# Padding a one-column constant from 4 to 128 bytes, so that the tiles behind it start on multiples of 128 bytes

## The chip, the cores and the metric

The kernel runs on one NeuronCore of a Trainium2 chip. What counts is device time in microseconds, as the median of the runs shown. The profile is of one further execution of the same program, so that execution has a time of its own. TensorE does the matmuls (PE, its weight loads PEld), VectorE (DVE) and ScalarE (ACT) do the arithmetic on whole tiles, GpSimd (POOL) a few normalisations and accumulating stores, and SyncE (SP) issues the other transfers.

## What is computed

Strided and local attention over 8 batches, 8 heads, 576 tokens and a head dimension of 64, and on its result a gated two-layer network with 4608 tokens, 512 model columns and 2048 hidden columns:

```python
scores = (q @ k.T) / sqrt(64)          # per batch and head
mask   = (0 <= i - j < 32) for heads 0..3
         (i >= j and i % 32 == j % 32) for heads 4..7
attn   = softmax(where(mask, scores, -1e9))
x      = (attn @ v) laid out as [4608 tokens, 512]
h      = x @ w_in                       # 512 -> 2048
g      = h * erf(softplus(h))
out    = g @ w_out                      # 2048 -> 512
```

## The kernel before, in words

The work is cut into 12 chunks of 384 tokens. For each chunk and each of 16 blocks of 128 hidden columns, `ftile` issues the first layer (`mm1`, line 678: 12 matmuls of 128x128 by 128x384 into `h`), a chain of ScalarE and VectorE steps for the gate (`n1` to `prod`, lines 686, 683 and 713), the split of the result into a high and a low part (`ghi` on ScalarE, line 716, and `glo` on VectorE, line 719), and the second layer (`mm2`, line 750: 9 matmuls of 128x128 by 128x512 into `o`). Both layers use the fp32r type with high and low parts, so each product is the sum of three matmuls. In the first layer the weight `pair` is the stationary operand and `xhi` or `xlo` streams past it; in the second `ghi` or `glo` is stationary and a weight `pair` streams. The profile writes the streaming operand first: `h<-xhi,pair` and `o<-pair,ghi`.

The attention of the eight batches (`heads`) is woven into this: scores on TensorE (line 400), softmax on the vector engines, transposes (line 507), the product with v (line 526), and the split of its result into `xhi` and `xlo` (lines 545 and 550). The order of all instructions is set when the program is built, by a planner (`Plan.order`) that looks at estimated durations and written keys, and not at addresses.

At the start the weights come in as 64-bit words of 4096 bytes per partition (`load` in `weight`, transfers `words<-w_in` and `words<-w_out`), beside the q, k and v of the first batches, which borrow the slots of weights that are needed later. While the first data comes in, a few matmuls on the constants (`warm`, line 863) keep TensorE occupied.

Memory in each partition of SBUF is handed out pool by pool, in the order in which tiles are asked for. The first pool, `cpool`, holds `xhi`, `xlo`, `ident`, `con` and last `con_e`; behind it lie `apool` (q, k, v, softmax tiles), `mpool` (`a`, `b`, `ghi`, `glo`, `ob`) and `wpool` (weights). `con_e` is one zero per partition: GpSimd sets it (line 793), and ScalarE takes its exponential (line 796) at the very start. No other instruction reads it.

Of the kernel before, what the change touches and what calls it, by code (L numbers as in the profile page):

```python
# [8 lines left out]
F32 = mybir.dt.float32  # L9
# [3 lines left out]
AF = mybir.ActivationFunctionType  # L13
# [5 lines left out]
P = 128  # L19
# [247 lines left out]
def attention_moe(  # L267
# [12 lines left out]
    nc = tc.nc  # L280
    PSUM = bass.MemoryType.PSUM

    cpool = ctx.enter_context(tc.tile_pool(name="cpool", bufs=1))
# [8 lines left out]
    xlo = [cpool.tile([P, RING], F32R, name=f"xlo{c}") for c in range(NCC)]  # L292
    ident = cpool.tile([P, P], F32, name="ident")
    con = cpool.tile([P, NCON], BF16, name="con")
    con_e = cpool.tile([P, 1], F32, name="con_e")
    mask_l = con[:, :320]
    mask_s = con[:, 320:384].rearrange("p (u q) -> p u q", u=1)
    ident_b = con[:, 384:]
# [491 lines left out]
        yield nc.sync.dma_start(ident, ident_f)  # L790

    def zero():
        yield nc.gpsimd.memset(con_e, 0.0)

    def first_exp():
        yield nc.scalar.activation(con_e, con_e, AF.Exp)

    o_con = [plan.add("sp", 0.35, -20.0, load_consts)]
    o_ident = plan.add("sp", 0.2, KI, load_ident)
    o = plan.add("pool", 0.1, -20.0, zero)  # L800
    plan.add("act", 1.6, -18.0, first_exp, [o])
    o_ps, order_o, stored = [None] * NTT, [None] * NTT, {}

# [161 lines left out]
```

## Time and profile before

| | |
|---|---|
| Median of the three runs | 931.43 us (lowest 930.68) |
| Profiled execution | 933.05 us, span 931.3 us |
| Mean granted TensorE clock | 0.993 |
| PE busy | 909.7 us, 98% of the span |
| DVE busy | 686.7 us, 74% |
| ACT busy | 653.4 us, 70% |
| POOL busy | 60.9 us, 7% |
| Moved by DMA | 68.86 MB in 23421 packets |

Three runs are in the list; one of them took 2283.8 us and stands far from the other two and from the profiled execution.

How to read the lines that follow: a group of instructions has its source line, engine, operation, the tile written, an arrow and the tiles read, then partitions by columns for output and input, the count, the busy time in us and the mean duration of one in ns, and last the idle time of the engine ahead of these instructions with what ended it. Matmuls run in a pipeline, so one may last longer than the step from its start to the start of the next. The span in slices gives a digit per fortieth of the span, 23.3 us each: 9 means busy for 90% or more.

### The profile page before, as it was taken

Reading aid. Unit: us, or ns where it says so; the run is one execution under the profiler, and the core shown is the slowest. Engines: PE = TensorE matmul, PEld = TensorE weight load, DVE = VectorE, ACT = ScalarE, POOL = GpSimd, SP = SyncE. Lnnn points to the kernel's source line nnn. Section 1 sums busy time; section 2 is a strip of 40 time slices with the busy share of each in tenths; the row PEclk is TensorE's granted clock in tenths of the full one; section 3 lists DMA queues with packets and bytes.
Section 4 is the critical chain, followed back from the end, with each engine's and each line's share of the span. In section 5 each row is a group of like instructions: output and inputs, shape, how many; then the busy total and the mean of one; then the engine's idle time right before and its main releaser. Section 6 shows DMA issues by size and latency. Waiting matters only on the chain.

```text
span 931.3 us, 20134 instructions
## 1 busy us (share of the span) xinstructions
PE 909.7 (98%) x8166; PEld 809.6 (87%) x8169; DVE 686.7 (74%) x1352; ACT 653.4 (70%) x1476; POOL 60.9 (7%) x59
## 2 busy tenths in 40 slices
PE   5789999999999999999999999999999999999998
PEld 4678888898888889988888899998898899999997
DVE  5999999996757766669886876667876666666664
ACT  5687887887776767667666666766766766766765
POOL 2200012110101100001110100000100000000000
PEclk9799999999999999999999999999999999999999
DMA  9994124321313010013312300002300200000000
GB/s 336 391 362 154 62 57 73 61 34 48 78 58 86 30 64 35 27 57 105 99 56 92 124 17 1 34 1 73 135 1 30 70 1 1 34 1 0 34 1 35
DMA packets 23421, 68.86 MB, mean 74 GB/s; under 512 B 2592, under 2 KB 3232, under 8 KB 23328
## 3 DMA queue, kind: packets, MB, share of 16 engines
q1 hardware_dynamic: 20736, 62.86, 18.9%
q0 software_dynamic: 2592, 4.72, 3.6%
q8 instruction: 64, 1.05, 0.5%
q14 instruction: 29, 0.24, 0.1%
HBM read 53.41 MB, written 14.16 MB: 73 GB/s over the span
## 4 chain that ended last, share of the span: by engine, by line
PE 90%; DVE 4%; ACT 3%; issue 1%; DMA 1%; SPq 0%; POOL 0%; ACTq 0%; POOLq 0%
PE h L678 41%; PE o L750 40%; PE s L400 3%; PE x L526 3%; PE t L507 2%; PE s L526 1%; DMA qk<-qk_loc 1%; ACT b L686 1%; DVE a L683 1%; DVE b L683 1%; ACT a L686 1%; PE s L507 1%; DVE glo L719 1%; ACT sm L472 0%; DVE h L713 0%
## 5 line engine op out<-in xcount | busy, mean ns | idle before, releaser
L750 PE MATMUL o<-pair,ghi 128*128 128x512 f32 x1152 | 361.4, 395 | 0.2 <-ACT ghi L716 0.2
L678 PE MATMUL h<-xhi,pair 128*128 128x384 f32 x1536 | 302.4, 339 | 0.6 <-DVE glo L719 0.6
L678 PEld LDWEIGHTS h<-xhi,pair 128*128 128x128 f32 x1536 | 271.4, 188 | 16.5 <-DVE glo L719 2.6
L686 ACT ACTIVATE b<-b 128x384 f32<-128x384 f32 x384 | 200.4, 522 | 77.2 <-DVE b L683 73.8
L750 PEld LDWEIGHTS o<-pair,ghi 128*128 128x128 f32 x1152 | 209.8, 188 | 32.4 <-ACT ghi L716 0.7
L750 PE MATMUL o<-pair,glo 128*128 128x512 f32 x576 | 224.8, 390 | 0.0
L683 DVE SCALAR_TENSOR_TENSOR a<-h,a 128x384 f32<-128x384 f32 x192 | 106.3, 553 | 83.3 <-ACT a L686 82.8
L678 PE MATMUL h<-xlo,pair 128*128 128x384 f32 x768 | 164.4, 336 | 0.0
L686 ACT ACTIVATE a<-h 128x384 f32<-128x384 f32 x192 | 93.5, 487 | 100.9 <-PE h L678 100.2
L683 DVE SCALAR_TENSOR_TENSOR a<-a,h 128x384 f32<-128x384 f32 x192 | 105.5, 549 | 68.9 <-ACT b L686 68.9
L713 DVE TENSOR_TENSOR h<-b,h 128x384 f32<-128x384 f32 x192 | 107.0, 557 | 46.2 <-ACT b L686 45.8
L678 PEld LDWEIGHTS h<-xlo,pair 128*128 128x128 f32 x768 | 136.0, 188 | 0.0
L750 PEld LDWEIGHTS o<-pair,glo 128*128 128x128 f32 x576 | 108.1, 188 | 23.7 <-DVE glo L719 0.3
L686 ACT ACTIVATE a<-a 128x384 f32<-128x384 f32 x192 | 100.3, 523 | 26.6 <-DVE a L683 26.1
L719 DVE TENSOR_TENSOR glo<-h,ghi 128x384 fp32r<-128x384 f32 x192 | 105.7, 550 | 11.7 <-ACT ghi L716 10.2
L716 ACT CAST ghi<-h 128x384 fp32r<-128x384 f32 x192 | 90.5, 471 | 29.1 <-DVE h L713 15.1
L683 DVE SCALAR_TENSOR_TENSOR b<-b,a 128x384 f32<-128x384 f32 x192 | 108.7, 566 | 1.0
L686 ACT ACTIVATE b<-a 128x384 f32<-128x384 f32 x192 | 101.0, 526 | 4.4
L498 POOL TENSOR_TENSOR sm<-sm,r 128x768 f32<-128x768 f32 (+3 forms) x36 | 45.0, 1249 | 435.3 <-DVE r L491 330.9
L436 DVE TENSOR_REDUCE mx<-s 128x12 f32<-128x768 f32 (+3 forms) x37 | 28.8, 784 | 10.6 <-PE s L413 10.3
L766 ACT COPY ob<-o 128x512 f32<-128x512 f32 x54 | 31.0, 588 | 2.7 <-PE o L750 2.2
L526 PEld LDWEIGHTS x<-pt,v 64*64 64x64 f32 x1392 | 24.4, 135 | 6.9 <-issue 4.4
(49 smaller groups left out, 511.4 us busy)
## 6 DMA issues: line engine op xcount, KB each, us to landing
out<-ob SPq DMA_DIRECT2D x36, 256.0 KB, 2.0
v<-v_loc SPq DMA_DIRECT2D x13, 640.0 KB, 4.1
words<-w_in SPq DMA_DIRECT2D x16, 512.0 KB, 8.6
words<-w_out SPq DMA_DIRECT2D x16, 512.0 KB, 9.1
qk<-qk_loc SPq DMA_DIRECT2D x13, 592.0 KB, 3.8
qk<-qk_str SPq DMA_DIRECT2D x12, 608.0 KB, 3.8
v<-v_str SPq DMA_DIRECT2D x16, 384.0 KB, 3.3
out<-ob POOLq DMA_DIRECT2D x18, 256.0 KB, 4.6
```

The source lines that it names most:

```text
L436: yield nc.vector.tensor_reduce(out=mx[:, parts[i], :units], in_=wide(of(s, i)), axis=mybir.AxisListType.X, op=ALU.max)
L498: yield (nc.gpsimd if pool_norm else nc.vector).tensor_tensor(out=d, in0=d, in1=spread(rc, i), op=ALU.mult)
L507: yield nc.tensor.transpose(bank(t, h)[:, 128 * w : 128 * w + 128], sm[:, h, c : c + 128], ident)
L526: yield nc.tensor.matmul(bank(px, m)[h * D : (h + 1) * D, a * n : (a + 1) * n], values(rows, (2 * a + h) * D), pt[rows, h, c : c + n], sta ...
L678: yield nc.tensor.matmul(ph[:, :CH], win[4 * s + cc][:, w, fs], x[cc][:, c0 : c0 + CH], start=(i == 0), stop=(i == len(terms) - 1))
L683: yield nc.vector.scalar_tensor_tensor(out=out, in0=in0, scalar=scalar, in1=in1, op0=op0, op1=op1)
L686: yield nc.scalar.activation(dst, src, func, bias=bias[i], scale=scale)
L713: yield nc.vector.tensor_tensor(out=ph[:, :CH], in0=bb.tile, in1=ph[:, :CH], op=ALU.mult)
L716: yield nc.scalar.copy(ghi.tile, ph[:, :CH])
L719: yield nc.vector.tensor_tensor(out=glo.tile, in0=ph[:, :CH], in1=ghi.tile.bitcast(F32), op=ALU.subtract)
L750: yield nc.tensor.matmul(po.tile, g[:, ts], wout[f][:, w], start=(f == first_f and i == 0), stop=(f == last_f and i == 2),)
L766: yield nc.scalar.copy(ob.tile, po.tile)
```

## The change

`con_e` is declared with 32 columns of four bytes, and its two users take the first column, as before:

```diff
-    con_e = cpool.tile([P, 1], F32, name="con_e")
+    con_e = cpool.tile([P, 32], F32, name="con_e")
...
-        yield nc.gpsimd.memset(con_e, 0.0)
+        yield nc.gpsimd.memset(con_e[:, :1], 0.0)
...
-        yield nc.scalar.activation(con_e, con_e, AF.Exp)
+        yield nc.scalar.activation(con_e[:, :1], con_e[:, :1], AF.Exp)
```

The order of instructions is the same on every engine. The addresses are not: four bytes took 32 in the pool, now they take 128, and everything behind `con_e` stands 96 bytes further on. From the two built programs, byte address within the partition:

| Tile | before | past a multiple of 128 | now | past a multiple of 128 |
|---|---|---|---|---|
| `xhi` (first), read by the first layer | 16512 | 0 | 16512 | 0 |
| `ident` | 53376 | 0 | 53376 | 0 |
| `con` | 53888 | 0 | 53888 | 0 |
| `con_e` | 54912 | 0 | 54912 | 0 |
| `sm` (first) | 54944 | 32 | 55040 | 0 |
| `mx` (first, second buffer) | 61088, 61152 | 32, 96 | 61184, 61248 | 0, 64 |
| `qk` (first) | 61216 | 32 | 61312 | 0 |
| `a` (first) | 83616 | 32 | 83712 | 0 |
| `ghi` (first) | 89760 | 32 | 89856 | 0 |
| `glo` (first) | 92832 | 32 | 92928 | 0 |
| first weight slot (`words`, `pair`) | 95904 | 32 | 96000 | 0 |

All other tiles behind `con_e` go from 32 to 0 as well, but for the second buffer of `r`, which goes from 96 to 64 like that of `mx`. The weight slots, 4096 bytes each, stood 160 bytes past a multiple of 256 and now stand on one; `con` stands 128 past a multiple of 256 in both kernels. Tiles in PSUM stay where they were.

## The prediction

> **What bounds the kernel now.** I read the page from the top: busy shares first, then the span in slices, then the chain that ended last.
>
> ```profile
> PE 909.7 (98%) x8166; PEld 809.6 (87%) x8169; DVE 686.7 (74%) x1352; ACT 653.4 (70%) x1476; POOL 60.9 (7%) x59
> PE   5789999999999999999999999999999999999998
> PEclk9799999999999999999999999999999999999999
> DMA  9994124321313010013312300002300200000000
> PE 90%; DVE 4%; ACT 3%; issue 1%; DMA 1%; SPq 0%; POOL 0%; ACTq 0%; POOLq 0%
> PE h L678 41%; PE o L750 40%; PE s L400 3%; PE x L526 3%; PE t L507 2%; PE s L526 1%; DMA qk<-qk_loc 1%; ACT b L686 1%; DVE a L683 1%; DVE b L683 1%; ACT a L686 1%; PE s L507 1%; DVE glo L719 1%; ACT sm L472 0%; DVE h L713 0%
> ```
>
> TensorE is busy for 98% of the span and is 90% of the chain; its two large matmul groups, the first layer (h, line 678) and the second layer (o, line 750), are 81% of it. Only the first three slices look different: the DMA engines are full there and TensorE is not. The table by stretch gives that in numbers (columns: length, busy time and count for each engine, granted clock, DMA share, GB/s).
>
> ```profile
> 0.00:23.30 23.30, 13.98 (x378) 9.36 (x382) 13.02 (x33) 12.04 (x51) 5.34 (x10) 1.00 0.94 336
> 23.30:46.60 23.30, 18.24 (x429) 15.44 (x421) 21.08 (x49) 15.28 (x64) 4.78 (x6) 0.71 1.03 391
> 46.60:69.90 23.30, 20.89 (x340) 16.95 (x341) 22.57 (x51) 19.01 (x59) 1.94 (x2) 1.00 0.93 362
> 69.90:500.00 430.10, 429.24 (x3895) 383.44 (x3894) 345.90 (x674) 314.68 (x671) 37.89 (x34) 1.00 0.24 66
> 500.00:931.30 431.30, 427.35 (x3143) 384.41 (x3142) 284.15 (x549) 292.44 (x632) 10.94 (x8) 1.00 0.10 35
> ```
>
> TensorE idles 9.32 + 5.06 + 2.41 = 16.8 us in the first 69.9 us, and only 0.86 + 3.95 = 4.8 us in the remaining 861.4 us. So an address can matter to the time in two places: how fast TensorE reads its operands, everywhere, and how fast the DMA engines write, in the first 69.9 us.
>
> **The change, part by part.** No instruction is added, removed or moved on any engine; the memset and the exponential on the constant keep their one column. What changes is where in its partition each tile of the three later pools starts: 32 bytes past a multiple of 128 before, on it now. I call that remainder the phase. The x tiles, ident and con have phase 0 in both kernels, so the kernel before already holds operands of both kinds, and the trace can be asked to compare them.
>
> *TensorE, moving operand.* The first layer streams x (phase 0), the second streams w_out pairs (phase 32). From the steady part, in order of time (start, length, operation):
>
> ```profile
> 801.09 1.55 PE L678 MATMUL h<-xhi,pair 128*128 128x384 f32 x8
> ...
> 803.18 0.62 PE L750 MATMUL o<-pair,ghi 128*128 128x512 f32 x2
> ...
> 805.22 1.55 PE L678 MATMUL h<-xhi,pair 128*128 128x384 f32 x8
> ```
>
> Twelve first-layer matmuls pass from 801.09 to 803.18, 2.09 us or 174 ns each; nine second-layer ones from 803.18 to 805.22, 2.04 us or 227 ns each. The 128 columns more cost 53 ns, or 0.414 ns a column; 384 columns are then 159 ns and 512 are 212 ns, and each kind has about 15 ns left over. The group that streams from phase 0 carries the same surplus as the group that streams from phase 32. Realigning the moving operand is worth 0.
>
> *TensorE, stationary operand.* Here all large matmuls have phase 32 (weight pairs, ghi, glo), so the pair above cannot decide. The small attention matmuls can. The weight loads of line 526 (v, 64 columns) all start at phase 32. The 64-column ones of line 400 (strided queries) start at multiples of 216 bytes from phase 32, and so at phases 0, 8, 16, 32, 40, 48, 56, 80, 88, 96 and 120.
>
> ```profile
> L526 PEld LDWEIGHTS x<-pt,v 64*64 64x64 f32 x1392 | 24.4, 135 | 6.9 <-issue 4.4 <-ACT b L686 0.7 <-ACT pt L513 0.7
> L400 PEld LDWEIGHTS s<-qk 64*64 64x64 f32 x576 | 9.5, 134 | 3.8 <-issue 1.4 <-ACT pt L513 1.2 <-PE o L750 0.7
> L400 PEld LDWEIGHTS s<-qk x1616: 102/107/136, 15.1 to 677.9; 64*32 64x32 f32 x115, 64*64 64x64 f32 x65
> ```
>
> The mean is 134 ns with all phases mixed and 135 ns with phase 32 alone. The third row gives minimum, median and maximum over all loads of that line: none takes over 136 ns, so no phase costs more than a nanosecond over another. Sorted by phase, leaving out the first ten of each group, the 48 loads at phase 0 have a mean of 135.0 ns and those at 16 and 40 of 135.1. I take 0 for this part too. One end stays open: these loads are plain fp32 and 64 columns wide, the large ones are fp32r and 128 wide. The far end is the first rival below.
>
> *VectorE and ScalarE.* The twins are the two splits into high and low parts: xlo and xhi live at phase 0, glo and ghi at phase 32.
>
> ```profile
> L719 DVE TENSOR_TENSOR glo<-h,ghi 128x384 fp32r<-128x384 f32 x192 | 105.7, 550 | 11.7 <-ACT ghi L716 10.2
> L550 DVE TENSOR_TENSOR xlo<-x,xhi 128x320 fp32r<-128x320 f32 x12 | 5.8, 481 | 0.0
> L550 DVE TENSOR_TENSOR xlo<-x,xhi 128x256 fp32r<-128x256 f32 x12 | 5.1, 424 | 6.7 <-ACT xhi L545 6.5
> L716 ACT CAST ghi<-h 128x384 fp32r<-128x384 f32 x192 | 90.5, 471 | 29.1 <-DVE h L713 15.1 <-PE o L750 13.3 <-PE h L678 0.3
> L545 ACT CAST xhi<-x 128x320 fp32r<-128x320 f32 x12 | 5.2, 430 | 0.0
> L766 ACT COPY ob<-o 128x512 f32<-128x512 f32 x54 | 31.0, 588 | 2.7 <-PE o L750 2.2 <-DMA out<-ob 0.3
> ```
>
> On VectorE the aligned rows grow by 57 ns for 64 columns, so 384 aligned columns would take 538 ns, against 550 unaligned: at most 12 ns, 2%, in favour of alignment. On ScalarE the unaligned rows grow by 117 ns for 128 columns, so 320 unaligned columns would take 412 ns, against 430 aligned: the other sign. Neither is a phase effect that I would bill. At most, 2% of VectorE's 4% of the chain (37 us) is 0.8 us; 18 ns of 412 is 4.4%, and on ScalarE's 3% (28 us) that is 1.2 us lost. Both engines wait for others for a quarter of the span, which hides the rest. Taken: 0.
>
> *DMA.* 25 MB land in the first 69.9 us, worked out from the three rates in the stretches above, most of it in tiles that move. Three issues can be compared:
>
> ```profile
> qk<-v_loc SPq DMA_DIRECT2D x3, 128.0 KB, 7.6
> con<-consts SPq DMA_DIRECT2D x1, 128.0 KB, 3.9
> ident<-ident_f SPq DMA_DIRECT2D x1, 64.0 KB, 7.2
> ```
>
> The first two rows are four transfers of 128 packets of 1024 bytes each, three into phase 32 and one into phase 0. Sorted by size, the packet records have a median of 46 ns for both kinds. The 4480 packets of 4096 bytes, all to or from moved tiles, have a median of 159 ns. That is 0.0368 ns a byte and 8.3 ns a packet, and from this line the 512-byte packets of ident (phase 0) should take 27 ns, which is what all 128 of them take. So phase 0 and phase 32 lie on one line. Taken: 0.
>
> [...]
>
> *Sum.* The profiled execution took 933.05 us, 1.75 us beyond its span of 931.3; plus 0 for TensorE, 0 for the vector engines, 0 for DMA, it is 933.05 us. The median of the runs is 931.43 us, 1.6 us (0.17%) lower, and a measurement of this kernel cannot tell less than about 2% from no change. I predict the median, **931.4 us**.
>
> **The rivals.**
>
> *The stationary operand does pay (faster).* The warm-up matmuls are bf16 with everything at phase 0 and 512 columns:
>
> ```profile
> 11.35 1.46 PE L863 MATMUL warm<-con 128*128 128x512 bf16 x6
> L863 PE MATMUL warm<-con x22: 379/379/635, 5.6 to 59.4; 128*128 128x512 bf16 x22
> ```
>
> Six in 1.46 us, the last one 379 ns long: (1460 - 379) / 5 = 216 ns from start to start, 11 ns less than the second layer. If those 11 ns were the price of an unaligned stationary tile, 1536 + 768 + 1152 + 576 = 4032 large matmuls would give back 44 us: 887 us. The counts have these rows:
>
> ```profile
> L750 PE MATMUL o<-pair,ghi 128*128 128x512 f32 x1152 | 361.4, 395 | 0.2 <-ACT ghi L716 0.2
> L678 PE MATMUL h<-xhi,pair 128*128 128x384 f32 x1536 | 302.4, 339 | 0.6 <-DVE glo L719 0.6
> L750 PE MATMUL o<-pair,glo 128*128 128x512 f32 x576 | 224.8, 390 | 0.0
> L678 PE MATMUL h<-xlo,pair 128*128 128x384 f32 x768 | 164.4, 336 | 0.0
> L863 PEld LDWEIGHTS <-con 128*128 128x128 bf16 x25 | 2.6, 106 | 7.7 <-DMA con<-consts 5.6 <-issue 0.8
> L678 PEld LDWEIGHTS h<-xhi,pair 128*128 128x128 f32 x1536 | 271.4, 188 | 16.5 <-DVE glo L719 2.6
> ```
>
> For it: no fp32r matmul with an aligned stationary tile exists here, and the surplus is the same for both layers, which share just that. Against it: the 64-column loads, which do not care; and the last two rows, where a bf16 load takes 106 ns and an fp32r load of as many columns 188 ns. The two kinds differ in how they load whatever their phase, so the type is enough to explain 11 ns.
>
> *The loading stage shrinks (faster, within 2%).* If the 8.3 ns that each packet costs beyond its bytes were the price of its phase, a 4096-byte packet would fall by 8.3 of 159 ns, 5.2%, and the 69.9 us by 3.6 us: 927.8 us. Even with all 16.8 us of idle TensorE gone it is 914.6 us, still within 2%. The 46 ns and the 27 ns speak against it. [...]
>
> *Equal phases collide (slower).* Now x and the weight pairs, which line 678 reads at once, have one phase where they had two. If reads of one phase got in each other's way, all 2304 first-layer matmuls would pay. The nearest price is again the 11 ns between 227 and 216: 25 us, 957 us. It passes 2% (18.6 us) from 8 ns a matmul on. Against it: the second layer already reads two operands of one phase (pair and ghi, both 32), and has no more surplus than the first.
>
> *The change does not do what it says.* Only if the pools did not move; the addresses in the section on the change show that they do. The second buffers of mx and r go from phase 96 to 64, not 0, but they hold 48 bytes for small vector steps.
>
> **How the numbers follow.** No effect: 0.85, at 931.4. A shorter loading stage: 0.08, 914.6 to 929.5. The stationary operand pays: 0.04, 887. Collision: 0.03, 957. The last two alone leave the 2% band: faster 0.04, same 0.93, slower 0.03. The range takes the likeliest case with its bounds: below, the lowest run (930.68) less 3.6 us of loading, 927.1; above, the profiled execution (933.05) plus the 1.2 us of ScalarE and as much scatter as the readings have among themselves (2.4 us), 936.6.
>
> **What would show it.** In the profile after, the first layer should still step by 174 ns and the second by 227 ns, weight loads should last 188 ns, glo 550 ns, ghi 471 ns, and 4096-byte packets 159 ns; the busy shares should agree to a digit. A second-layer step of 216 ns would prove the first rival, a first-layer step over 180 ns the collision, and DMA shares well under 0.93 in the first three slices the loading rival. I am wrong if 128-column fp32r loads know a phase that 64-column ones do not.

## The result, and the profile after

The changed kernel's median is 936.28 us, against 931.53 us for the kernel before on the same chip: ratio 1.0056, 95% interval [1.0036, 1.0075]. It is slower by half a per cent, and clearly so. The ratio is that of the means, without the one run of 2283.8 us of the kernel before. Its profiled execution took 936.42 us, with a span of 934.7 us.

From the page after, busy shares and the span in slices:

```profile
PE 913.7 (98%) x8166; PEld 812.6 (87%) x8169; DVE 687.6 (74%) x1352; ACT 654.2 (70%) x1476; POOL 61.0 (7%) x59
PEclk9799999999999999999999999999999999999999
DMA  9993224321313010013213300002300200000000
```

The first three stretches of the changed kernel:

```profile
0.00:23.30 23.30, 14.98 (x407) 10.04 (x409) 13.60 (x34) 12.31 (x52) 5.48 (x10) 1.00 0.92 341
23.30:46.60 23.30, 17.45 (x482) 15.32 (x485) 21.52 (x50) 16.51 (x66) 4.65 (x5) 0.78 1.03 404
46.60:69.90 23.30, 20.92 (x263) 17.01 (x257) 23.20 (x53) 18.70 (x60) 1.94 (x2) 1.00 0.92 365
```

TensorE is busy for 4.0 us more; the vector engines for 0.9 and 0.8 us. The groups show the same: the operations that I had compared by phase did not move, the matmuls did.

```profile
L750 PE MATMUL o<-pair,ghi 128*128 128x512 f32 x1152 | 363.6, 397 | 0.3 <-ACT ghi L716 0.2
L678 PE MATMUL h<-xhi,pair 128*128 128x384 f32 x1536 | 304.5, 340 | 0.3 <-DVE glo L719 0.3
L678 PE MATMUL h<-xlo,pair 128*128 128x384 f32 x768 | 165.9, 338 | 0.0
L678 PEld LDWEIGHTS h<-xhi,pair 128*128 128x128 f32 x1536 | 273.0, 188 | 15.6 <-DVE glo L719 1.5
L719 DVE TENSOR_TENSOR glo<-h,ghi 128x384 fp32r<-128x384 f32 x192 | 105.8, 551 | 11.8 <-ACT ghi L716 10.4
L716 ACT CAST ghi<-h 128x384 fp32r<-128x384 f32 x192 | 90.7, 472 | 28.9 <-DVE h L713 15.0 <-PE o L750 13.7
```

The place of the loss is the step from one matmul to the next. One block of the changed kernel in order of time:

```profile
803.54 1.57 PE L678 MATMUL h<-xhi,pair 128*128 128x384 f32 x8
804.95 0.86 PE L678 MATMUL h<-xlo,pair 128*128 128x384 f32 x4
805.65 0.63 PE L750 MATMUL o<-pair,ghi 128*128 128x512 f32 x2
806.12 0.39 PE L750 MATMUL o<-pair,glo 128*128 128x512 f32 x1
806.35 0.62 PE L750 MATMUL o<-pair,ghi 128*128 128x512 f32 x2
806.80 0.39 PE L750 MATMUL o<-pair,glo 128*128 128x512 f32 x1
807.02 0.62 PE L750 MATMUL o<-pair,ghi 128*128 128x512 f32 x2
807.48 0.39 PE L750 MATMUL o<-pair,glo 128*128 128x512 f32 x1
807.71 1.57 PE L678 MATMUL h<-xhi,pair 128*128 128x384 f32 x8
```

The twelve first-layer matmuls take 805.65 - 803.54 = 2.11 us, 0.02 more than before. Of the second layer only the first two steps are longer (806.12 - 805.65 = 0.47 us for two, against 806.80 - 806.35 = 0.45 for the next such pair). The block takes 4.17 us instead of 4.13. In the trace's records of single instructions, to the nanosecond, the median of the 128 blocks whose 21 matmuls follow each other with no other matmul between them goes from 4127 to 4160 ns.

The loss builds up evenly. The 21st block starts 1.6 us earlier than before (135.07 against 136.66 us), so the loading stage of this execution was shorter. From there on each of the remaining 171 blocks costs 29 ns more (4590 against 4561 ns, with all that lies between them), 5.0 us. Less 1.6 that is the 3.4 us between the spans.

### The profile page after: what moved, and what is told of

Same layout as the page of the kernel before. It is cut to its first block, busy times and chain, and to the rows that moved or that the text cites. A ratio compares the mean times of both kernels' runs of the same rounds, so it can differ in the third digit from the quotient of the medians.

```text
span 934.7 us, 20134 instructions
## 1 busy us (share of the span) xinstructions
PE 913.7 (98%) x8166; PEld 812.6 (87%) x8169; DVE 687.6 (74%) x1352; ACT 654.2 (70%) x1476; POOL 61.0 (7%) x59
## 4 chain that ended last, share of the span: by engine, by line
PE 86%; issue 7%; DVE 3%; DMA 2%; ACT 1%; SPq 1%; POOL 0%; ACTq 0%; POOLq 0%
PE h L678 39%; PE o L750 39%; PE x L526 3%; PE s L400 3%; PE t L507 2%; DMA qk<-qk_loc 1%; DMA out<-ob 1%; PE s L526 1%; DVE a L683 1%; PE s L507 1%; ACT b L686 0%; DVE b L683 0%; DVE pair L649 0%; DVE glo L719 0%; DVE w L635 0%
```

## Experiments

The steps of a matmul went up although no other engine did more. I held three theories: **(1)** the operand that TensorE streams and the stationary one that it loads at the same time get in each other's way, depending on where both start; **(2)** stationary tiles that start on a multiple of 128 are slow; **(3)** the vector engines' accesses get in the way of TensorE's when their tiles have the phase of x. Loads and matmuls do run at the same time: in the changed kernel PEld is busy for 812.6 us and PE for 913.7 us of a span of 934.7 us. In what follows the *distance* of a layer is the start of its stationary tile less the start of its streamed tile, modulo 256 bytes. It is 32 for the first and 0 for the second layer before, 128 and 0 after. All tiles that one layer uses in a role have the same remainder, since their sizes and slices are multiples of 256 or 512 bytes.

### Moving one set of tiles at a time

The weight slots alone (phase 0; q, k, v and gate tiles stay at 32):

```diff
+    gap = ctx.enter_context(tc.tile_pool(name="gap", bufs=1)).tile([P, 24], F32, name="gap")
     wpool = ctx.enter_context(tc.tile_pool(name="wpool", bufs=1))
```

> Only the weight slots move, from 32 past a multiple of 128 bytes to 0; q, k, v, softmax and gate tiles (ghi, glo among them) stay at 32, x at 0. Theory 1 (x and the first layer's weights, which TensorE reads at once, get in each other's way when they have one phase): first-layer step 175.5 ns instead of 173.5, the first two second-layer steps after it 234 and 233 instead of 228 and 227 as in the changed kernel, about 936 us. Theory 2 (weights at phase 0 are slow whatever x has): the same. Theory 3 (the vector engines' tiles at the phase of x disturb TensorE): 173.5 ns, about 930 us. The loading stage should end 1.5 us earlier in all three if the writes to the weight slots gain from phase 0.

Measured: 1.0114 [1.0099, 1.0128]. First-layer steps went to 175.8 ns, as in the changed kernel (175.5), but all nine second-layer steps grew, to 232.9 ns on average, which no theory had foreseen. No single set of tiles was responsible for a fixed price.

The attention and gate tiles alone (`con_e` with 32 columns, and a gap of 8 columns ahead of `wpool`):

> Only the tiles of attention and gate move to phase 0 (ghi and glo among them); the weight slots stay at 32 past a multiple of 128 (288 instead of 160 past one of 512), x at 0. Theory 1 and theory 2: first-layer step 173.5 ns, about 931.5 us. Theory 3: 175.5 ns, about 936 us. No gain in the loading stage if it comes from the weight slots.

Measured: 1.011 [1.0093, 1.0127]; 176.4 and 231.9 ns. Here x and the weights keep their phases, and the first layer is slower than in any run so far. Phases modulo 128 are not the right quantity; the weights' remainder of 256 changed.

x, ident and con alone (`con_e` asked for ahead of `xhi`, the rest as before), and the same with everything else at phase 0 (24 columns of padding behind `con` besides):

```diff
+    con_e = cpool.tile([P, 1], F32, name="con_e")
     xhi = [cpool.tile([P, RING], F32R, name=f"xhi{c}") for c in range(NCC)]
...
-    con_e = cpool.tile([P, 1], F32, name="con_e")
```

> Only the x tiles, ident and con move, from phase 0 to 32; everything else stays at 32. x and the weights then have one phase, but it is 32 and not 0. Theory 1: first-layer step 175.5 ns, about 937 us. Theory 2: 173.5 ns, 931.5 us. Theory 3 (equal phase of x and the gate tiles): 175.5 ns.

> x, ident and con at phase 32, everything else at 0: the mirror of the kernel before. Theory 1: first-layer step 173.5 ns, and with the earlier end of loading 930 us. Theory 2: 175.5 ns, 936 us. Theory 3: 173.5 ns, 930 us.

Measured: 1.0082 [1.0066, 1.0098] and 1.0038 [1.0025, 1.0051]. With x at 32 the first layer slowed to 175.2 ns, as theory 1 had it, but the second slowed too, to 231.3 ns, though it does not read x. In the mirror layout the weights are at phase 0 and the first layer has its 173.7 ns, which ends theory 2. The second layer has 231.2 ns there, so the time is not that of before.

### How far the pattern reaches

The same gap with 32 columns (weights 128 bytes further), `con_e` with 40 columns (all behind it 128 further), and with 136 columns (512 further):

> Only the weight slots move, by 128 bytes: all tiles keep their remainder of 128 (x 0, the rest 32), but the weights' remainder of 512 goes from 160 to 288. If only remainders of 128 count, steps stay at 173.5 and 227 ns and the time at that of before. If more of the address counts, steps grow, as they did in the run that moved the tiles of attention and gate alone: 176 and 232 ns, about 943 us.

> Everything behind the constant moves by 128 bytes together; remainders of 128 as before, x unmoved. If only remainders of 128 count: time of before, steps 173.5 and 227 ns. If the distance between x and the weights counts beyond 128 bytes: first-layer step up by 2 ns and second-layer steps up after it, 936 us or more.

> Everything behind the constant moves by 512 bytes; remainders of 512 as before. If the pattern repeats within 512 bytes: time of before, within 0.2%, steps 173.5 and 227 ns. If it doesn't (or if any other layout than the one tuned for is worse for a reason that is not the address), slower by about 0.5 to 1%.

Measured: 1.0118 [1.01, 1.0136], 1.0101 [1.0085, 1.0117] and 0.9996 [0.9986, 1.0006]. A shift of 512 bytes changes nothing, one of 128 costs 1%: more of the address than its remainder of 128 counts, and a whole 512 does not.

### TensorE by itself

The loop of the short kernel, with the names of its variables shortened:

```python
for n in (384, 512):
    for m in range(16):
        for s in range(16):
            matmul(mark, half[:, :128], half)             # one bf16 matmul between groups
            for r in range(24):
                matmul(y[:, :n], sta[:, 8*s + 128*(r%4) :][:, :128], mov[:, 8*m + 512*(r%2) :][:, :n])
```

> Leaves out the whole computation: no attention, no gate, nothing on VectorE or ScalarE while TensorE runs. It streams fp32r matmuls of 384 and then 512 columns, each with its own weight load, in groups of 24 at one pair of starts, the streamed operand at 16 starts 32 bytes apart and the stationary one at 16, so 256 pairs for each length, with one bf16 matmul between groups. Theory 1 (the two operands that TensorE reads at once get in each other's way, by where each starts): the step differs between pairs by some ns, as the program's 173.5 to 176 and 227 to 232 ns do, and the map shows after how many bytes it repeats. Theory 3 (reads and writes of the vector engines get in TensorE's way): 173.3 and 226.7 ns for all 256 pairs. Theory 2 (the stationary start alone counts): the step changes along the stationary starts only.

Four groups of it in order of time, 24 matmuls of 512 columns each, with a streamed start of 0; the stationary start goes from 64 to 192, 224 and 256 bytes:

```profile
1156.38 5.95 PE L43 MATMUL y<-mov,sta 128*128 128x512 f32 x24
...
1179.69 5.85 PE L43 MATMUL y<-mov,sta 128*128 128x512 f32 x24
...
1185.42 5.96 PE L43 MATMUL y<-mov,sta 128*128 128x512 f32 x24
...
1191.26 5.83 PE L43 MATMUL y<-mov,sta 128*128 128x512 f32 x24
```

The groups differ by 0.13 us, with nothing else running (one execution, granted clock 1.00). From the records, the mean of the last 15 steps of a group, over the groups of one distance (the very first group left out):

| Distance, bytes | 0 | 32 | 64 | 96 | 128 | 160 | 192 | 224 |
|---|---|---|---|---|---|---|---|---|
| 384 columns, ns | 173.3 | 173.3 | 173.3 to 176.7 | 173.3 | 176 | 177 | 173.3 | 173.3 to 176.9 |
| 512 columns, ns | 226.9 | 233.4 | 233.4 | 234.3 | 232.4 | 233.4 | 228.9 | 233.4 |

All pairs of starts with one distance lie within 0.7 ns of each other, but for the two cells that give a range. So it is the distance that counts, it repeats after 256 bytes, and theory 3 is not needed. In those two cells the distance alone does not decide: at 64, for instance, the groups have 173.3, 174.7 or 176.6 ns, by where the pair starts. None of the layouts here has a first layer at 64 or 224. The first layer after the change (distance 128) and with only the weights moved (128) is at 176, the second layer of the latter (160) at 233.

What this table, made of the last 15 steps of each group, does not give is the second layer at distance 0, which had 227 ns in some programs and 231 in others. So TensorE ran whole blocks of twelve and nine matmuls, for 8 by 8 distances.

> Leaves out the whole computation. TensorE alone runs the kernel's block order, twelve first-layer and nine second-layer matmuls, five blocks for each of 64 pairs of distances (stationary start less streamed start, 0 to 224 bytes in steps of 32, for either layer). If the distances alone decide, each layer's steps are those of the map of single pairs whatever the other layer does: second layer at distance 0 always 226.7 ns. If what ran before also decides (the runs with distance 0 in the second layer had 227 ns in three programs and 231 ns in three others), the second layer at distance 0 has 227 ns after a first layer at 32 or 128 and 231 ns after one at 0, 96 or 160.

Blocks with distances 32 and 0 (before), and with 128 and 0 (after):

```profile
185.40 2.25 PE L47 MATMUL y<-xt,wt 128*128 128x384 f32 x12
187.48 2.20 PE L49 MATMUL o<-wt,gt 128*128 128x512 f32 x9
189.53 2.25 PE L47 MATMUL y<-xt,wt 128*128 128x384 f32 x12
```

```profile
693.13 2.27 PE L47 MATMUL y<-xt,wt 128*128 128x384 f32 x12
695.24 2.22 PE L49 MATMUL o<-wt,gt 128*128 128x512 f32 x9
697.29 2.27 PE L47 MATMUL y<-xt,wt 128*128 128x384 f32 x12
```

Start to start, 4.13 and 4.16 us: the difference of the two kernels, without the kernels. What ran before does count: at distance 0 the second layer has 227 ns after a first layer at 32, 64 or 224 and 228 after one at 128 or 192, but 231 after one at 0, 96 or 160. After a first layer at 128 its steps are 234, 233, 228 and then about 227 ns: the two long steps of the changed kernel, whose second layer is at distance 0 as it was before. My expectation named 0, 96 and 160 rightly; for 128 it had 227.

The records of the single pairs show what the 231 ns are, which their last 15 steps hide. Of the 32 groups with 512 columns at distance 0, 31 are uneven in their first five to nine steps (224 to 236 ns) and only then settle at 227. One begins, after the gap behind the bf16 matmul, with 229, 233, 236, 224, 231, 236, 228, 233 and 231 ns, and stays at 226 or 227 from there on. These are, within a nanosecond, the nine steps that the second layer has in the program with x at 32. So 231 ns is not a second steady step at distance 0: it is a start, paid anew in every block, that takes as long as a layer of nine matmuls. It goes the other way too: in blocks with both distances at 0 the first layer has early steps of up to 185 ns, though the table has 173.3 at its distance, and in the program with x at 32 it had 175.2.

### Three more layouts

All large tiles 96 bytes further than before, x included (`con_e` with 24 columns ahead of `xhi`, and 8 columns of padding behind `con`). This is the changed kernel with x, ident and con moved by 96:

> The changed kernel with x, ident and con moved by 96 bytes too, so that every large tile stands 96 bytes further on than before: all distances between tiles as before, and the weights, q, k, v and gate tiles on multiples of 128 as in the changed kernel. If distances decide on TensorE and multiples of 128 on the transfers: steps 173.9 and 227.7 ns, the loading stage 1.6 us shorter, about 1.5 us faster than before (0.998). If the multiple of 128 itself were what slows TensorE: 175.5 ns and the changed kernel's time, 1.005.

Measured: 0.9991 [0.9981, 1.0001]; steps 173.9 and 227.8 ns, as before. So for TensorE nothing is wrong with multiples of 128; the change lost its time by moving the weights without x. A block of this layout in order of time:

```profile
802.32 1.55 PE L678 MATMUL h<-xhi,pair 128*128 128x384 f32 x8
...
804.40 0.62 PE L750 MATMUL o<-pair,ghi 128*128 128x512 f32 x2
804.86 0.39 PE L750 MATMUL o<-pair,glo 128*128 128x512 f32 x1
...
806.45 1.55 PE L678 MATMUL h<-xhi,pair 128*128 128x384 f32 x8
```

It takes 806.45 - 802.32 = 4.13 us, and the first two steps of its second layer are back at 804.86 - 804.40 = 0.46 us. The gain that I expected in the loading stage can neither be told from nothing nor ruled out: the interval holds 1 and also the 0.998 that I named for it (1.5 us of 932 are 0.9984). This is its second stretch:

```profile
23.30:46.60 23.30, 18.64 (x387) 16.15 (x386) 20.55 (x48) 15.25 (x63) 4.63 (x5) 0.58 1.02 397
```

The granted clock was 0.58 there, against 0.71 before and 0.78 after, and the 21st block started at 137.44 us, later than in both.

Two layouts chosen from the map, one bad and one good (`con_e` with 16 columns and a gap of 8 ahead of `wpool`; `con_e` with 48 columns):

> A layout that was not run yet: weights 96 bytes past x and ghi, glo 224 past the weights (by remainders of 256); first-layer distance 96, second-layer distance 224. By the blocks that TensorE ran alone this is among the worst of the 64 pairs, 4220 ns a block against 4127 for the distances of before. The seven programs with other distances grew by about 0.8 of what their blocks alone say, so 75 ns a block, 192 blocks, 14.4 us: about 946 us, ratio 1.015. If multiples of 128 decide instead, no tile that moves is on one here: time of before.

> First-layer distance 192, second-layer distance 0: the second best of the 64 pairs, 4133 ns a block alone against 4127. Expected 5 ns a block, 1 us in all: about 933 us, ratio 1.001. All tiles that move stand 64 past a multiple of 128; if a step away from the layout of before costs for itself, 1.005 or more.

Measured: 1.0072 [1.0056, 1.0088] and 0.9997 [0.9988, 1.0005]. The second came out as expected. The first is slower, but by half of what I said: of its 128 blocks in the program 105 take 4173 or 4174 ns, and only 7 the 4220 ns that they have alone. Both times stand in one trace, at the same addresses; what chooses between them is not shown.

All layouts together, block times from the records:

| Layout | Distances | Block alone, ns | Median in the program, ns | Ratio to before |
|---|---|---|---|---|
| before | 32, 0 | 4127 | 4127 | 1 |
| all by 512 | 32, 0 | 4127 | 4127 | 0.9996 |
| all by 96, x too | 32, 0 | 4127 | 4127 | 0.9991 |
| distance 192 | 192, 0 | 4133 | 4133 | 0.9997 |
| **after** | 128, 0 | 4160 | 4160 | 1.0056 |
| x at 32, rest at 0 | 96, 0 | 4167 | 4167 | 1.0038 |
| x at 32 | 0, 0 | 4187 | 4187 | 1.0082 |
| attention and gate alone | 160, 224 | 4200 | 4200 | 1.0110 |
| all by 128 | 160, 0 | 4200 | 4200 | 1.0101 |
| weights alone | 128, 160 | 4204 | 4205 | 1.0114 |
| weights by 128 | 160, 128 | 4213 | 4213 | 1.0118 |
| bad pair | 96, 224 | 4220 | 4173 | 1.0072 |

In eleven of the twelve programs the block has the time that TensorE shows alone, within a nanosecond. No pair of the 64 is below 4127 ns, and no layout tried beats the kernel before by more than its interval.

## Why the prediction was wrong, step by step

**Bound: right.** TensorE's stream of matmuls sets the time (PE is busy for 98% of the span in both kernels), and the loss is in it.

**Moving operand, 0: wrong, and this is the step that failed.** I compared a group that streams from phase 0 with one that streams from phase 32, found the same 15 ns of surplus in both, and concluded that the start does not matter. That comparison could not have come out otherwise: the 0.414 ns a column were taken from the same two steps as the surpluses, and a straight line through two points leaves both the same rest, whatever disturbs either. As the map shows, both groups were at distances, 32 and 0, where TensorE alone has its shortest steps (173.3 and 226.9 ns), so neither was a disturbed case. And I judged each operand by itself: x, which the first layer streams, did not move at all, and its matmuls slowed because the weights loaded beside it moved. The change took the first layer to distance 128: 173.9 to 175.5 ns over all its steps after 80 us, 2304 times 1.6 ns or 3.7 us. The second layer went from 227.7 to 228.9 ns, 1728 times 1.2 ns or 2.1 us. That is 5.8 us, of which 5.0 us show between the 21st block and the end.

**Stationary operand, 0: right for what the rows showed, and too narrow.** A weight load of the first layer takes 188 ns at phase 32 before and at phase 0 after. The loss is not in the duration of the load but in the step of the matmuls.

**Vector engines, 0: right.** 550 and 551 ns for glo, 471 and 472 for ghi.

**DMA, 0: the row that I read was too coarse.** The median of 4096-byte packets is 159 ns in both kernels, but the share that takes just that went from 52% to 93%, and the mean from 170.4 to 166.3 ns. With the weights on a multiple of 128 the share is 93% in every layout, elsewhere 45% to 56%; the means lie closer together, 166.3 to 168.7 against 168.5 to 172.2 ns. The loading stage was 1.6 us shorter in the profiled execution after, but two expectations that hung on the weights' writes came out crosswise. With the weights alone on multiples of 128 the 21st block started at 135.77 us, 0.9 us earlier than before, and with the weights off such multiples, in the run that moved attention and gate alone, at 134.39 us, 2.3 us earlier. The second stretch of that run:

```profile
23.30:46.60 23.30, 15.30 (x484) 13.62 (x467) 21.67 (x50) 16.54 (x67) 4.64 (x5) 0.85 1.03 399
```

The three earliest (this one, the mirror layout with 134.40 us, and the changed kernel) are those with the highest granted clocks in the second stretch, 0.85, 0.78 and 0.78; the other nine had 0.57 to 0.71. So the shorter stage goes with the clock rather than with the share of short packets. Each is one execution, and the cause stays open.

**Sum: its remark on precision was wrong.** I held that less than 2% cannot be told from no change. The interval [1.0036, 1.0075] tells half a per cent.

**The rivals.** "Equal phases collide" named the right two operands and the right sign, at 0.03, with a wrong condition and price. Not equal phases but the distance modulo 256 decides (the second layer has equal phases and, before, 227.7 ns), and it costs 2 ns and not 11. I had priced it by the surplus of an fp32r over a bf16 step, which is there at every distance (216 ns a step in the warm-up, 226.9 to 234.3 ns in the table), and gave no weight to a collision of a nanosecond or two, of which 4032 matmuls make half a per cent. The first rival and the loading rival did not happen at their prices. The median of 936.28 us lies near the upper end of the range, for a reason that had no part in it.

## What to carry to other kernels

A tile's address can cost time without any instruction changing: in a stream of fp32r matmuls the distance between the tile that is streamed and the tile that is loaded next to it, modulo 256 bytes, was worth up to 3% of a step (226.9 to 234.3 ns with 512 columns, 173.3 to 177 ns with 384). So a change that shifts only some tiles (a pad, a new constant, another pool order) should be judged by the distances it changes, and measured. When a trace is to show that something does not matter, one must know that the cases compared differ in the thing that matters; two short kernels, one that sweeps both starts and one that keeps the order of the blocks, did in two runs what ten layouts did not.

## What the runs showed of the hardware

- With nothing else running, an fp32r matmul of 384 or 512 columns with its own weight load starts every 173.3 or 226.9 ns at the best distance between the starts of its two operands, and every 177 or 234.3 ns at the worst. In the two kernels the first layer's step was 173.9 ns at distance 32 and 175.5 ns at 128. The runs show the dependence, not what causes it.
- What ran before counts for several matmuls. At distance 0 the steps of 512 columns settle at 227 ns, but in 31 of 32 groups only after five to nine uneven ones of up to 236 ns. The second layer has nine matmuls, so it averaged 227 or 231 ns by the distance of the first. At distances 96 and 224 blocks of 4173 and of 4220 ns stand in one trace; why is not shown.
